# Attention: the value products in two row halves of 64 keys, set apart between the score products

## The chip, the cores and the metric

The kernel runs on one core of one Trainium2 chip. The metric is the time of one execution on the device, in microseconds, as the median of several runs. Engines are named as in the profile: PE is TensorE (PEld its weight loads), DVE is VectorE, ACT is ScalarE, POOL is GpSimd, SP is SyncE, which issues most of the DMAs.

## The reference, cut to what matters

```python
def _A_ref(x, wqkv, wo):                    # B=1, S=2048, D=640
    H = 32
    Dh = D // H                             # 20
    q, k, v = ...                           # x @ wqkv, each [B, H, S, Dh]
    scores = jnp.einsum("bhqd,bhkd->bhqk", q, k) * (Dh ** -0.5)
    p = _softmax(scores, axis=-1)
    o = jnp.einsum("bhqk,bhkd->bhqd", p, v)
    return (...o as [B, S, D]...) @ wo

x = A_x
h = x + _A_ref(_layernorm(x, axis=-1), A_wqkv, A_wo)
h2 = h + _B_ref(_layernorm(h, axis=-1), B_w_gate, B_w_up, B_w_down)   # swiglu, F=1728
```

All is float32. The change touches the attention alone, from the scores to the sums of `p` times `v`.

## The kernel before, in words

The program has three parts: layer norm with the q, k and v projections; attention; the output projection, second layer norm and feed-forward part. Some work of the third part (splitting weights on POOL, the first output projections) is put between attention steps.

Attention takes four heads at a time (`G = 4`, eight groups) and 512 queries at a time, which makes 32 *units* (`NU`). A unit goes over the 2048 keys in 16 *steps* of 128 keys, so there are 512 steps. Two heads are stacked on the rows of a tile: head rows 0 to 61 are the lower row half (`b = 0`), rows 64 to 125 the upper one (`b = 1`). A head has 20 columns; a product of 60 rows takes three pairs of split parts (high and low) of them at once, and two more rows subtract the maximum.

What a step does, by the names in the code:

- `scores` (L1290, L1296): four products of 62 rows by 512 queries, `s` for the lower row half and `S` for the upper. Each fills one PSUM bank (`ps_one`), and ACT takes the exponential of it into `probs`.
- `max_one` (L261, L267) and `max_start` (L289, L298): the maxima of the scores for a *later* unit. `m` and `M` are single products of 60 rows by 512 keys on one row half, each followed by a DVE reduction of its bank (`ps_max`). `x` and `X` are the two parts, 256 keys each, of one shared item: the lower half in `x`, the upper in `X` of the same step, into one bank, with one reduction for both after `X`. Of the items a third is shared (`EVERY = 3`). About 490 of the 512 steps have maxima to do; the last twenty or so have none left.
- `weigh` (L1300), called `W`: the sums of `probs` times values for the step two before, four heads in four column blocks of 32, over all 128 keys in one go. They are float32 products; the program holds four, and the chip runs eight instructions. They add up over a unit's 16 steps in one bank, `acc`.

The order of these operations on PE is written out by hand in a string, `ORDER = "WxnSmSsMXs"`; `n` is a marker on ACT that issues no work. Steps without maxima use `"sSsSW"`. There is no scheduler: each engine gets its instructions in the order of the code.

PSUM has eight banks: one for `acc`, four for scores (`ps_one` goes round two of the pool `psum_two` and two of the pool `psum`), three for maxima (`ps_max`).

At the end of a unit, which is in the second step of the next one, `row_sums` copies `acc` to SBUF on ACT (L1310) and sends its row sums off by DMA; the reciprocals and the scaling follow some steps later on DVE and POOL. `max_all` (L309) reduces the found maxima of a unit to one column, `found_of` (L277) makes the tile for them.

Of the kernel before, what the change touches and what calls it, by code (L numbers as in the profile page):

```python
# [9 lines left out]
F32 = mybir.dt.float32  # L10
# [7 lines left out]
P = 128  # L18
# [6 lines left out]
NT = S // P  # L25
# [15 lines left out]
ORDER = "WxnSmSsMXs"  # L41
# [7 lines left out]
EXTRA = 2  # L49
EVERY = 3  # L50
# [3 lines left out]
def tile_block(ctx: ExitStack, tc: tile.TileContext, x, wqkv, wo, wg, wu, wd, out):  # L54
# [218 lines left out]
    def found_of(u):  # L273

        if u not in found:
            f = found[u] = pp.tile([P, 2, 2, TPC, NC + EXTRA], F32, name="found", tag="found", bufs=3)
            nc.vector.memset(f[:, :, :, :, NC:], LOWEST)  # L277
# [4 lines left out]
    def max_start(u, kc, t, pair, half, column):  # L282

        ps = ps_max()

        def part(b):
            rows = slice(b * ROW, b * ROW + NPART)
            first = kc * CH + half * CH // 2
            nc.tensor.matmul(  # L289
                ps[:, b * CH // 2 : (b + 1) * CH // 2],  # L290
                queries[u][rows, pair, t * P : (t + 1) * P],
                keys[u // NC][rows, pair, first : first + CH // 2],
                start=(b == 0), stop=True, skip_group_check=True,
            )

        def last():
            part(1)
            nc.vector.tensor_reduce(  # L298
                found_of(u)[:, :, pair, t, column], ps.rearrange("p (b n) -> p b n", b=2),
                axis=AX.X, op=ALU.max,  # L300
            )

        part(0)
        return lambda: nc.scalar.clobber_nop([nc.scalar.lower_ap(ps)]), last
# [71 lines left out]

    plain_items, shared = [], []
    used = {}
    for n, (u, kc, t, pair) in enumerate(rest):
        if n % EVERY:  # L380
            plain_items.append((u, kc, t, pair))
        else:
            extra = NC + used.setdefault((u, t, pair), 0)
            used[u, t, pair] += 1
            shared += [(u, kc, t, pair, 0, kc), (u, kc, t, pair, 1, extra)]
    assert max(used.values()) <= EXTRA

# [910 lines left out]
    def weigh(u, kt, probs, acc):  # L1298
        for j in range(G):
            nc.tensor.matmul(  # L1300
                acc[32 * j : 32 * j + 32, :],
                values[u // NC][:, kt, j * VW : j * VW + 32],
                probs[j // 2][:, j % 2, :],
                start=(kt == 0), stop=(kt == NT - 1),
                tile_position=(0, 32 * j),
            )

    def row_sums(acc, *queues):
        o = pc.tile([P, CH], F32, name="o", bufs=2)
        nc.scalar.activation(o, acc, AF.Copy)  # L1310
# [36 lines left out]
    def counted(u):  # L1347
        left[u] -= 1
        if left[u] == 0:
            max_all(u)  # L1350
            if early_end(u):
                turn_maxima(u)
            closing[u] = now[0] + 2

    def next_max(b):
        if singles[b]:
            a = singles[b].pop(0)
            max_one(*a)
            counted(a[0])

    def next_shared(b):
        if b == 0 and shared:
            a = shared.pop(0)
            begun.append((a[0], *max_start(*a)))
        elif b == 1 and begun:
            u, _, last = begun.pop()
            last()
            counted(u)

    def weigh_next():  # L1370
        u, kt, probs = todo.pop(0)
        if kt == 0:
            accs[u] = psum.tile([P, CH], F32, name="acc", tag=f"ps_{last % 3}")
        weigh(u, kt, probs, accs[u])
        if kt == NT - 1:
            queues = [nc.sync] if u + 1 < NU else [nc.scalar, nc.sync]
            tail.append((u, *row_sums(accs.pop(u), *queues)))
# [3 lines left out]
    for u in range(NU):  # L1381
# [4 lines left out]
        for kt in range(NT):  # L1386
# [3 lines left out]
            order = ORDER if singles[0] or singles[1] or shared else "sSsSW"  # L1390
            place[0] += 1
            for op in order:
                if op in "mM":
                    next_max(int(op == "M"))
                elif op in "xX":
                    next_shared(int(op == "X"))
                elif op == "n":
                    if begun:
                        begun[0][1]()
                elif op in "sS":  # L1400
                    scores(u, kt, heads[op == "S"].pop(0), probs)
                else:
                    if len(todo) == 2:
                        weigh_next()
# [55 lines left out]
    while todo:  # L1460
        weigh_next()
# [562 lines left out]
```

## Time and profile before

| what | value |
|---|---|
| time, median of 2 runs | 2010.26 us (2009.89 to 2010.63) |
| the profiled execution | 2008.45 us, with a span of 2006.6 us |
| granted PE clock | 1.00 |
| PE busy | 99% of the span, 14792 instructions |
| PEld busy | 63% |
| DVE busy | 80%, 2873 instructions |
| ACT busy | 71%, 2833 instructions |
| POOL busy | 39% |
| DMA | 310.50 MB, mean 155 GB/s |
| first and last value product | 325.9 us and 1440.7 us after the start |

The attention steps thus fill some 1115 us of the 2006.6 us span. The ends of PE's products are modelled in the profile, so a PE that is shown 99% busy need not be at its peak; starts can be compared with each other. Two rows of one engine that overlap are pipelined: the next begins before the one ahead has ended.

### The profile page before, as it was taken

The numbers are of one execution on the slowest core, as the hardware profiler recorded it, in microseconds if no ns is written. First come the engines' busy times: TensorE is split into PE (matmuls) and PEld (weight loads), VectorE is DVE, ScalarE is ACT, GpSimd is POOL, SyncE is SP. The second block draws the span as 40 slices with busy tenths as digits, with TensorE's granted clock in tenths as the row PEclk, the third lists the DMA queues.
The fourth block names the chain that finished last, engine by engine and source line by source line (L and its number), as shares of the span: only waits on it lengthen the run. The fifth ranks groups of instructions, "written<-read, shape, count | busy, mean of one in ns | idle before, by whom it ended". The sixth has DMA issues, their size and how long they took to land.

```text
span 2006.6 us, 41982 instructions
## 1 busy us (share of the span) xinstructions
PE 1983.5 (99%) x14792; PEld 1261.6 (63%) x14792; DVE 1606.8 (80%) x2873; ACT 1433.0 (71%) x2833; POOL 784.4 (39%) x1147
## 2 busy tenths in 40 slices
PE   8999999999999999999999999999999999999998
PEld 6989996444444444444444444455688888888888
DVE  5687778999999999999999988975488666676667
ACT  4677778999999999999999999977633222212221
POOL 6564423243342343234342111011245544844465
PEclk9999999999999999999999999999999999999999
DMA  7787563442533443434334222221258645974542
GB/s 240 262 254 258 173 209 88 128 123 94 161 104 122 141 140 125 130 119 149 128 130 157 79 73 60 77 66 60 62 204 289 232 168 175 354 251 162 201 147 94
DMA packets 197066, 310.50 MB, mean 155 GB/s; under 512 B 51368, under 2 KB 85480, under 8 KB 195832
## 3 DMA queue, kind: packets, MB, share of 16 engines
q1 hardware_dynamic: 190264, 284.21, 43.7%
q0 software_dynamic: 6496, 23.60, 4.0%
q8 instruction: 118, 1.93, 0.4%
q14 instruction: 92, 0.75, 0.1%
q10 hardware_dynamic: 96, 0.00, 0.0%
HBM read 208.11 MB, written 99.19 MB: 153 GB/s over the span
## 4 chain that ended last, share of the span: by engine, by line
PE 88%; DMA 2%; DVE 1%; POOL 1%; issue 1%; ACT 0%; SPq 0%; DVEq 0%; ACTq 0%; POOLq 0%
PE acc L1300 25%; PE ps_a L1487 15%; PE ps_one L1290 12%; PE ps_max L289 9%; PE ps_b L1581 8%; PE ps_max L261 7%; PE ps_one L667 7%; PE ps_max L228 2%; PE ps_max L1021 2%; PE ps_b L1021 1%; DMA o_t<-o_d 0%; DMA units<-w_d 0%; DMA halves<-j_d 0%; DMA t_d<-kept 0%; PE ps_max L1056 0%
## 5 line engine op out<-in xcount | busy, mean ns | idle before, releaser
L1296 ACT ACTIVATE probs<-ps_one 128x512 f32<-128x512 f32 x2048 | 1048.9, 616 | 44.1 <-PE ps_one L1290 34.8
L267 DVE TENSOR_REDUCE found<-ps_max 128x1 f32<-128x512 f32 x980 | 630.5, 685 | 83.3 <-PE ps_max L261 63.7
L1290 PE MATMUL ps_one<-q_stk,k_stk 62*128 62x512 f32 x2048 | 577.4, 428 | 1.1 <-DVE m L102 0.9
L1300 PE MATMUL acc<-probs,v_stk 128*32 128x512 f32 x4096 | 545.2, 604 | 0.0
L289 PEld LDWEIGHTS ps_max<-k_stk,q_stk 60*128 60x128 f32 x984 | 181.8, 185 | 407.2 <-DVE found L267 400.3
L261 PE MATMUL ps_max<-k_stk,q_stk 60*128 60x512 f32 x980 | 392.7, 422 | 0.0
L298 DVE TENSOR_REDUCE found<-ps_max 128x2 f32<-128x512 f32 x492 | 335.3, 682 | 0.0
L289 PE MATMUL ps_max<-k_stk,q_stk 60*128 60x256 f32 x984 | 324.1, 329 | 0.0
L1290 PEld LDWEIGHTS ps_one<-q_stk,k_stk 62*128 62x128 f32 x2048 | 303.1, 184 | 25.3 <-ACT probs L1296 19.5
L1702 DVE TENSOR_TENSOR tmp<-ps_a,tmp 128x512 f32<-128x512 f32 x208 | 141.2, 689 | 120.4 <-PE ps_a L1487 93.6
L250 DVE TENSOR_REDUCE mx<-ps_max 128x2 f32<-128x512 f32 x288 | 180.4, 685 | 63.9 <-PE ps_max L228 60.0
L261 PEld LDWEIGHTS ps_max<-k_stk,q_stk 60*128 60x128 f32 x980 | 181.0, 185 | 50.2 <-DVE found L298 21.9
L240 ACT ACTIVATE ps_max<-ps_max 128x512 f32<-128x512 f32 x288 | 151.6, 583 | 46.4 <-PE ps_max L228 43.7
L1581 PE MATMUL ps_b<-halves,yp 128*128 128x320 f32 x1032 | 179.3, 308 | 2.0 <-DMA halves<-j_d 1.2
L1581 PEld LDWEIGHTS ps_b<-halves,yp 128*128 128x128 f32 x1032 | 165.1, 188 | 18.6 <-POOL yp L102 1.5
L1487 PE MATMUL ps_a<-t,units 128*128 128x512 f32 x624 | 162.5, 396 | 0.0
L1300 PEld LDWEIGHTS acc<-probs,v_stk 128*32 128x32 f32 x4096 | 80.6, 108 | 127.6 <-issue 118.5
L1487 PE MATMUL ps_a<-z,units 128*128 128x512 f32 x516 | 133.8, 394 | 0.0
L102 POOL TENSOR_TENSOR yp<-y,yp 128x256 fp32r<-128x256 f32 x96 | 60.4, 629 | 187.8 <-ACT yp L101 187.8
L1487 PEld LDWEIGHTS ps_a<-t,units 128*128 128x128 f32 x624 | 112.6, 188 | 18.6
L1335 POOL TENSOR_TENSOR o<-o,rb 128x512 f32<-128x512 f32 x31 | 40.0, 1289 | 200.9 <-DMA rb<-r_d 94.7
L1586 DVE TENSOR_TENSOR h<-ps_b,h 128x320 f32<-128x320 f32 x248 | 109.9, 480 | 6.9 <-PE ps_b L1581 5.4
(220 smaller groups left out, 2977.7 us busy)
## 6 DMA issues: line engine op xcount, KB each, us to landing
units<-w_d SPq DMA_DIRECT2D x186, 256.0 KB
w_d<-stage SPq DMA_DIRECT2D x106, 256.0 KB
halves<-j_d SPq DMA_DIRECT2D x70, 320.0 KB
j_d<-stage SPq DMA_DIRECT2D x42, 320.0 KB
k_stk<-k_d SPq DMA_DIRECT2D x64, 160.0 KB
q_stk<-q_d SPq DMA_DIRECT2D x64, 160.0 KB
raw<-k_d SPq DMA_DIRECT2D x62, 160.0 KB
raw<-q_d SPq DMA_DIRECT2D x54, 160.0 KB
```

The source lines that it names most:

```text
L240: nc.scalar.activation(ps, ps, AF.Relu)
L250: nc.vector.tensor_reduce(mx[:, b, :, t, kc], ps.rearrange("p (j n) -> p j n", j=2), axis=AX.X, op=ALU.max,)
L261: nc.tensor.matmul(ps, queries[u][rows, pair, t * P : (t + 1) * P], keys[u // NC][rows, pair, kc * CH : (kc + 1) * CH], start=True, stop=True,
L267: nc.vector.tensor_reduce(found_of(u)[:, b, pair, t, kc : kc + 1], ps, axis=AX.X, op=ALU.max)
L289: nc.tensor.matmul(ps[:, b * CH // 2 : (b + 1) * CH // 2], queries[u][rows, pair, t * P : (t + 1) * P], keys[u // NC][rows, pair, first : ...
L298: nc.vector.tensor_reduce(found_of(u)[:, :, pair, t, column], ps.rearrange("p (b n) -> p b n", b=2), axis=AX.X, op=ALU.max,)
L1290: nc.tensor.matmul(ps, keys[u // NC][rows, p, kt * P : (kt + 1) * P], queries[u][rows, p, :], start=True, stop=True,)
L1296: nc.scalar.activation(probs[p][:, b, :], ps, AF.Exp, scale=scale)
L1300: nc.tensor.matmul(acc[32 * j : 32 * j + 32, :], values[u // NC][:, kt, j * VW : j * VW + 32], probs[j // 2][:, j % 2, :], start=(kt == 0) ...
L1487: nc.tensor.matmul(ps.rearrange("p (t n) -> p t n", t=TPC), w[k][:, i], z[k][:, :, j], start=(first and m == 0), stop=(last and m == len(n ...
L1581: nc.tensor.matmul(ps, a, b, start=(n == 0), stop=(n == len(pairs) - 1))
L1702: add = lambda out, ps, x: nc.vector.tensor_tensor(out=out, in0=ps, in1=x, op=ALU.add)
```

## The change

Three things change together, all in the attention.

1. `weigh` gets a row half `b`. Its products take 64 keys instead of 128, and a second call does the other 64. `v` in the new order strings is the lower half, `w` the upper. The two halves add up in banks of their own, `acc0` and `acc1`, and `row_sums` adds the two on DVE after ACT's copy.
2. The shared items with their two parts of 256 keys go. All maxima are single products of 512 keys again, three in each step. The order string becomes two, for even and odd steps.
3. The second bank of sums is taken from the scores, which then have three banks; the maxima keep three.

```diff
-ORDER = "WxnSmSsMXs"
+ORDERS = ("SMvSswmsm", "smwsvSMSM")
...
-EXTRA = 2
-EVERY = 3
...
     def ps_one():
-        n = turn[0] % 4
+        n = turn[0] % 3
         turn[0] += 1
         if n < 2:
             return psum_two.tile([P, CH], F32, name="ps_one", tag="ps_two")
-        return psum.tile([P, CH], F32, name="ps_one", tag=f"ps_{(last + n - 1) % 3}")
+        return psum.tile([P, CH], F32, name="ps_one", tag=f"ps_{(last + 1) % 3}")
...
-    def weigh(u, kt, probs, acc):
+    def weigh(u, kt, probs, acc, b):
+        rows = slice(b * ROW, (b + 1) * ROW)
         for j in range(G):
             nc.tensor.matmul(
                 acc[32 * j : 32 * j + 32, :],
-                values[u // NC][:, kt, j * VW : j * VW + 32],
-                probs[j // 2][:, j % 2, :],
+                values[u // NC][rows, kt, j * VW : j * VW + 32],
+                probs[j // 2][rows, j % 2, :],
                 start=(kt == 0), stop=(kt == NT - 1),
-                tile_position=(0, 32 * j),
+                tile_position=(b * ROW, 32 * j),
             )
 
     def row_sums(acc, *queues):
         o = pc.tile([P, CH], F32, name="o", bufs=2)
-        nc.scalar.activation(o, acc, AF.Copy)
+        nc.scalar.activation(o, acc[0], AF.Copy)
+        nc.vector.tensor_tensor(out=o, in0=acc[1], in1=o, op=ALU.add)
...
-    singles = [[(*a, b) for a in plain_items] for b in range(2)]
-    begun = []
+    singles = [[(*a, b) for a in rest] for b in range(2)]
...
-    def weigh_next():
-        u, kt, probs = todo.pop(0)
-        if kt == 0:
-            accs[u] = psum.tile([P, CH], F32, name="acc", tag=f"ps_{last % 3}")
-        weigh(u, kt, probs, accs[u])
+    weighing = []
+
+    def weigh_next(b):
+        if not weighing:
+            weighing.append((todo.pop(0), {0, 1}))
+        (u, kt, probs), halves = weighing[0]
+        halves.remove(b)
+        if kt == 0 and len(halves) == 1:
+            accs[u] = [
+                psum.tile([P, CH], F32, name=f"acc{i}", tag=f"ps_{(last + 2 * i) % 3}")
+                for i in range(2)
+            ]
+        weigh(u, kt, probs, accs[u][b], b)
...
-            order = ORDER if singles[0] or singles[1] or shared else "sSsSW"
-            place[0] += 1
+            order = ORDERS[kt % 2] if singles[0] or singles[1] else "sSvsSw"
```

How this moves the instructions is seen best in the order in which they stand. First PE, in the middle of the attention, before: a little over one step. Each row is a line of the kernel, an operation and its tiles, with its count where rows repeat; `acc` is the bank of sums, `ps_one` a bank of scores, `ps_max` a bank of maxima.

```order
L1300 MATMUL acc<-probs,v_stk_146 32x512 x4
L289 MATMUL ps_max<-k_stk_145,q_stk 128x256
L1290 MATMUL ps_one<-q_stk,k_stk_145 128x512
L261 MATMUL ps_max<-k_stk_145,q_stk 128x512
L1290 MATMUL ps_one<-q_stk,k_stk_145 128x512 x2
L261 MATMUL ps_max<-k_stk_145,q_stk 128x512
L289 MATMUL ps_max<-k_stk_145,q_stk 128x256
L1290 MATMUL ps_one<-q_stk,k_stk_145 128x512
L1300 MATMUL acc<-probs,v_stk_146 32x512 x4
```

In a step before, the four value products stand together once, and eight score and maximum products stand between two such groups; the second of the two 256-key parts (L289) stands *ahead* of the step's last score product (L1290).

Now PE at the same place in the changed kernel, a little over one step, from the first value half of an even step on. L1252 is the score product, L259 the maximum, L1263 the value product; `acc_14219` is a unit's `acc0` (lower rows), `acc_14220` its `acc1` (upper rows).

```order
L1263 MATMUL acc_14219<-probs,v_stk_5610 32x512 x4
L1252 MATMUL ps_one<-q_stk,k_stk_5609 128x512 x2
L1263 MATMUL acc_14220<-probs,v_stk_5610 32x512 x4
L259 MATMUL ps_max<-k_stk_145,q_stk 128x512
L1252 MATMUL ps_one<-q_stk,k_stk_5609 128x512
L259 MATMUL ps_max<-k_stk_145,q_stk 128x512
L1252 MATMUL ps_one<-q_stk,k_stk_5609 128x512
L259 MATMUL ps_max<-k_stk_145,q_stk 128x512
L1263 MATMUL acc_14220<-probs,v_stk_5610 32x512 x4
L1252 MATMUL ps_one<-q_stk,k_stk_5609 128x512
L1263 MATMUL acc_14219<-probs,v_stk_5610 32x512 x4
```

The value products now stand in two groups of four in each step. The two groups of the upper rows have five products of the lower rows between them (L259 and L1252 in turn), and the two groups of the lower rows likewise have upper ones.

The second place is DVE at the end of a unit, where `o` is the tile that `row_sums` fills, `neg` the unit's maxima and `r` the row sums. Before:

```order
L267 TENSOR_REDUCE found<-ps_max 128x1 x2
L298 TENSOR_REDUCE found<-ps_max 128x2
L329 STREAM_TRANSPOSE turned<-both 128x32
L267 TENSOR_REDUCE found<-ps_max 128x1 x2
L298 TENSOR_REDUCE found<-ps_max 128x2
L267 TENSOR_REDUCE found<-ps_max 128x1 x2
L298 TENSOR_REDUCE found<-ps_max 128x2
```

and in the changed kernel:

```order
L282 TENSOR_REDUCE neg<-found 128x16
L265 TENSOR_REDUCE found<-ps_max 128x1 x4
L302 STREAM_TRANSPOSE turned<-both 128x32
L1274 TENSOR_TENSOR o<-acc_11927,o 128x512
L265 TENSOR_REDUCE found<-ps_max 128x1 x11
L1285 RECIPROCAL r<-r 128x16
L265 TENSOR_REDUCE found<-ps_max 128x1 x37
```

DVE keeps three reductions a step, all of one column now, and gets one addition for each unit (L1274) that stands in the row of reductions; in the second step of a unit one reduction is ahead of it and two are behind it.

More of the change, by code (lines that the diff above doesn't have):

```diff
@@ L275, in found_of @@
         if u not in found:
-            f = found[u] = pp.tile([P, 2, 2, TPC, NC + EXTRA], F32, name="found", tag="found", bufs=3)
-            nc.vector.memset(f[:, :, :, :, NC:], LOWEST)
+            f = found[u] = pp.tile([P, 2, 2, TPC, NC], F32, name="found", tag="found", bufs=3)
             if u in mxs:
@@ L280, in found_of @@
         return found[u]
[L282 to L304, printed above, removed]
     def max_all(u):
@@ L374, in tile_block @@
     ]
[L377 to L386, printed above, removed]
     evp_ctx = ExitStack()
@@ L1358, in next_max @@
             max_one(*a)
[L1359 to L1368, printed above, removed]
-    def weigh_next():
-        u, kt, probs = todo.pop(0)
-        if kt == 0:
-            accs[u] = psum.tile([P, CH], F32, name="acc", tag=f"ps_{last % 3}")
-        weigh(u, kt, probs, accs[u])
-        if kt == NT - 1:
-            queues = [nc.sync] if u + 1 < NU else [nc.scalar, nc.sync]
-            tail.append((u, *row_sums(accs.pop(u), *queues)))
+            u = a[0]
+            left[u] -= 1
+            if left[u] == 0:
+                max_all(u)
+                if early_end(u):
+                    turn_maxima(u)
+                closing[u] = now[0] + 2
+    weighing = []
[10 more added lines that the diff above has]
+        weigh(u, kt, probs, accs[u][b], b)
+        if not halves:
+            weighing.pop()
+            if kt == NT - 1:
+                queues = [nc.sync] if u + 1 < NU else [nc.scalar, nc.sync]
+                tail.append((u, *row_sums(accs.pop(u), *queues)))
     extra = []
@@ L1402, in tile_block @@
                 else:
-                    if len(todo) == 2:
-                        weigh_next()
+                    if len(todo) == 2 or weighing:
+                        weigh_next(int(op == "w"))
+                    if not once:
+                        continue
+                    once = False
                     for v, at in closing.items():
@@ L1460, in tile_block @@
     while todo:
-        weigh_next()
+        weigh_next(0)
+        weigh_next(1)
     u, o, r = tail.pop()
```

13 lines of the change are left out of this document (1 added, 12 removed).

## The prediction

> **What bounds the kernel now.** I read first the page's busy times, then a window over the attention steps, then the order of time of one step, then the groups and waits. Only the steps with maxima are looked at: 490 of the 512, since 980 single maxima go two to a step.
>
> ```profile
> PE 1983.5 (99%) x14792; PEld 1261.6 (63%) x14792; DVE 1606.8 (80%) x2873; ACT 1433.0 (71%) x2833; POOL 784.4 (39%) x1147
> L261 PE MATMUL ps_max<-k_stk,q_stk 60*128 60x512 f32 x980 | 392.7, 422 | 0.0
> 400.00:1300.00 900.00, 899.75 (x6875) 378.28 (x6871) 824.22 (x1409) 889.25 (x1754) 284.11 (x474) 1.00 0.39 118
> 400.00:1300.00 900.00, 877.51 (x1715) 1.00 0.39 118
> ```
>
> The third row is the window from 400 to 1300 us (busy time and count of PE, PEld, DVE, ACT, POOL), the fourth the same for the exponentials alone. Over the whole program ACT is 71% busy; in this window it is 889 of 900 us, DVE 824 and PE all of it. The whole-span shares hide that three engines are nearly full here. The 1715 exponentials, four to a step, make a step 900 × 4 / 1715 = **2.10 us**, and a unit of 16 steps 33.6 us.
>
> Which of the three is the bound? PE in order of time (start, length):
>
> ```profile
> 699.55 0.61 PE L1300 MATMUL acc<-probs,v_stk 128*32 128x512 f32 x4
> 700.10 0.38 PE L289 MATMUL ps_max<-k_stk,q_stk 60*128 60x256 f32 x1
> ...
> 701.22 1.07 PE L1300 MATMUL acc<-probs,v_stk 128*32 128x512 f32 x8
> 702.21 0.38 PE L289 MATMUL ps_max<-k_stk,q_stk 60*128 60x256 f32 x1
> 702.22 0.49 PE L1290 MATMUL ps_one<-q_stk,k_stk 62*128 62x512 f32 x1
> 702.44 0.40 PE L261 MATMUL ps_max<-k_stk,q_stk 60*128 60x512 f32 x1
> 702.55 0.52 PE L1290 MATMUL ps_one<-q_stk,k_stk 62*128 62x512 f32 x2
> 702.78 0.41 PE L261 MATMUL ps_max<-k_stk,q_stk 60*128 60x512 f32 x1
> 702.91 0.39 PE L1290 MATMUL ps_one<-q_stk,k_stk 62*128 62x512 f32 x1
> 703.03 0.27 PE L289 MATMUL ps_max<-k_stk,q_stk 60*128 60x256 f32 x1
> 703.24 1.06 PE L1300 MATMUL acc<-probs,v_stk 128*32 128x512 f32 x8
> 704.23 0.39 PE L289 MATMUL ps_max<-k_stk,q_stk 60*128 60x256 f32 x1
> ```
>
> From one value group to the next, 701.22 to 703.24, is 2.02 us: 0.99 us from the group's start to the next product, and 1.03 us in which the two row halves work side by side. The 0.99 us is always there (703.24 to 704.23 again): PE's own, not a wait. The first row shows a group's second four; from it to the next product is 0.55 us, so a pass of four takes 0.44 us, two take 0.89, and about **0.10 us** is spent going over to products of another shape. On entry the same: the last score started at 702.91 and, at the ordinary spacing on one half (702.55 to 702.78, 0.23 to 0.24 us), left its half at 703.14; the group began at 703.24.
>
> So PE needs at least 2.02 us a step and a step takes 2.10: **PE is the bound**. ACT stands close behind:
>
> ```profile
> 1333.13 2.06 ACT L1296 ACTIVATE probs<-ps_one 128x512 f32<-128x512 f32 x4 [1.27 <-PE ps_one L1290]
> L1296 ACT ACTIVATE probs<-ps_one 128x512 f32<-128x512 f32 x1715 | 878.0, 616 | 10.8 <-PE ps_one L1290 2.6
> 700.75 1.29 DVE L267 TENSOR_REDUCE found<-ps_max 128x1 f32<-128x512 f32 x2
> L267 DVE TENSOR_REDUCE found<-ps_max 128x1 f32<-128x512 f32 x858 | 552.3, 685 | 73.7 <-PE ps_max L261 56.2
> ```
>
> Four exponentials end 2.06 us after the first begins, and one lasts 0.616, so they follow each other at (2.06 − 0.62) / 3 = 0.48 us: 1.92 us a step. Two reductions take 1.29 us at 0.685 each, a spacing of 0.605: three take 1.82 us.
>
> **The change, inside a unit.** PE, for one row half in two steps: four scores and three maxima at 0.235 us, two value groups at 0.89, and two changes of shape (the half's two groups stand next to each other) at 0.10: 7 × 0.235 + 1.78 + 0.20 = 3.63 us, **1.81 us a step** instead of 2.02, if one half's value group runs beside the other half's scores. No row of before shows 64-key groups or such mixed work, so the 0.89 is that of 128 keys (the same 512 columns and eight instructions). Below, it can be no less than half of that by the rows, if half the keys took half the time, and then PE is only further from being the bound; above, it is the full serial price, priced as a rival.
>
> PE's instruction count grows: 7 + 16 = 23 products a step, against 16. The densest row that I found,
>
> ```profile
> 218.00:228.00 10.00, 10.00 (x158) 9.90 (x157) 6.77 (x12) 7.65 (x16) 6.22 (x7) 1.00 0.65 203
> ```
>
> has 158 products with their weight loads in 10 us, 63 ns each: 23 take 1.46 us, inside 1.81. At nothing, then, though a burst of eight behind a late bank can push a score by up to 0.5 us.
>
> With PE at 1.81, ACT is late next: 64 exponentials at 0.48 and the copy at the same spacing make 31.2 us a unit, 1.95 a step. DVE: 48 reductions at 0.605 are 29.0 us, and its small work is
>
> ```profile
> L309 DVE TENSOR_REDUCE neg<-found 128x16 f32<-128x96 f32 x27 | 6.9, 254 | 0.9
> L1321 DVE RECIPROCAL r<-r 128x16 f32<-128x16 f32 x27 | 6.5, 243 | 0.0
> L329 DVE STREAM_TRANSPOSE turned<-both 128x32 f32<-128x32 f32 x20 | 4.0, 201 | 0.0
> ```
>
> with three smaller groups some 0.9 us a unit; the new addition is nearest to the feed-forward part's addition from PSUM of the same shape, 0.69 us (below). Sum 30.6 us. So with every bank free in time a unit takes 31.2 us instead of 33.6, a gain of 2.4.
>
> Three score banks instead of four: a bank is taken for 0.39 (product) and 0.62 (exponential) and, by the gaps in these rows, about 0.15 between them and to the next product, 1.2 us; three at 0.48 give 1.44. Enough, with 0.2 us to spare, as long as nothing ahead is late. With the cover gone, each 0.1 us of lateness beyond that goes to ACT whole.
>
> **The end of a unit.** Here the change adds a wait. Before, the copy costs this:
>
> ```profile
> 727.42 0.63 ACT L1310 ACTIVATE o<-acc 128x512 f32<-128x512 f32 x1
> 728.11 1.06 PE L1300 MATMUL acc<-probs,v_stk 128*32 128x512 f32 x8
> L1702 DVE TENSOR_TENSOR tmp<-ps_a,tmp x208: 673/691/693, 1489.8 to 1993.4; 128x512 f32<-128x512 f32 x104
> ```
>
> The copy ends at 728.05 and the next unit's first group starts 0.06 us later. In the changed kernel the second step of a unit runs (from its start): score 0, maximum 0.24, score 0.47, value group of the lower rows 0.80, ending with its pipeline at 1.86; copy to 2.53; addition to 3.27. The addition waits in DVE's queue with two of the step's reductions behind it, and those hold two of the three banks of maxima. DVE has finished the step's first reduction at about 1.35, so it stands idle some 1.2 us. Its slack in a unit is only 31.2 − 30.6 = 0.6. The maxima of the next step wait for those banks, and on PE the scores behind them. And the upper rows' first group of the new unit, which stands about 1.0 us into the third step (2.95), waits for the addition (3.3).
>
> I price this between nothing (31.2 us a unit) and twice the 1.4 us from group's end to addition's end, once for DVE and once for PE behind it (34.0). DVE's idle time less its slack alone gives 31.8. I take **1.5 us**, just over the one-way length, so 32.7 us a unit.
>
> Other moves, at nothing: the row-sum DMAs are issued behind the addition, 0.7 us later in SP's queue, with stores and later units' queries behind them; the reciprocals that need them stand three steps on, 6 us, and queries are loaded three units ahead, so both keep their cover. The memset of 85 ns a unit goes. The twenty-odd steps without maxima have the same products with groups halved; their score parts are short, and I put them at 0 ± 6 us (20 steps by a third of a group's 0.89).
>
> **Sum**: 490 / 16 = 30.6 units × (33.6 − 32.7) = 27.5 us, 2008.45 − 27.5 = 1981 against the profiled execution. The median is 1.8 us above that execution, so 1983. With the ends, 31.4 to 34.0 us a unit, the time would be 1943 to 2022; I use 1955 as the lower end, since no unit will be free of the wait.
>
> **Rivals.** *The shapes exclude each other.* If PE finishes all work of one shape, on both halves, before it begins another, nothing overlaps. In favour: 0.10 us is lost at each change of shape in the rows above. Against: there both sides of the change share rows, so they do not tell whether a half by itself may change. The price: in two steps six products stand one after another on the upper rows (1.41 us), a score on each half (0.24), five on the lower (1.18) and one more (0.24), with four groups at 0.99 and four entries at 0.10: 7.43 us, 3.71 a step. (3.71 − 2.10) × 490 = 789 us, so **2800 us**. It decides as soon as a group of one half cannot start while the other half streams. [...]
>
> *Products start strictly in the order of the program.* Then a half's product waits for the start of all ahead of it, other half or not. Followed through: S 0, M 0.24, v 0.24, s 1.22 with w, then m, s, m, s, m to 2.40, w 2.40, s 2.63, v 2.97, then S 3.39, M, S, M, and the next S at 4.33: 2.165 a step, +32 us, and with the unit's end on top up to +78: 2042 to 2088, about **2065 us**. Against it: in the fence above the score at 702.91 starts before the 256-key maximum at 703.03, which the program puts ahead of it; the maximum's half was still taken, and the score passed it. [...]
>
> *Nothing is won* because the wait at the unit's end takes all 2.4 us: 2010 us. It is the upper part of my own range.
>
> **How the numbers follow.** My forecast, halves that run independently with a unit at 31.4 to 34.0 us: 0.68. Strict order: 0.12. Shapes exclude each other: 0.16. Anything else near no change, such as the two halves' streams slowing each other by a tenth: 0.04. A measurement of this kernel tells about 2%, 40 us, from no change. Faster by more needs a unit under 32.3 us, a third of my case: 0.22. Slower by more: all of the exclusion, nearly all of strict order, and 0.02 of mine: 0.29. Between: 0.49. The range takes in my case and the strict order, 1955 to 2085, and leaves out the exclusion and the tails, together 0.2. My own case alone is 1955 to 2022.
>
> **What will show it.** Right: L1263 groups with starts inside the other half's L1252 and L259 rows; ordinary steps near 1.95 us with exponentials 0.48 apart; a step of over 2.5 us once a unit, at L1274, with DVE waiting for L1273. Wrong: no product between the starts of a group and 0.9 us later (exclusion); scores never ahead of an earlier product of the other half (strict order); ACT idle within units, waiting for scores (too few banks).

## The result, and the profile after

The changed kernel takes **4436.49 us**, before 2010.26 us: a ratio of 2.207 (95% interval 2.197 to 2.216). The page of the changed kernel, with the row of the granted clock in 40 slices:

```profile
span 4434.6 us, 48244 instructions
PE 4411.8 (99%) x18396; PEld 1958.3 (44%) x18396; DVE 1713.0 (39%) x2874; ACT 1583.1 (36%) x2833; POOL 778.8 (18%) x1147
PEclk9995555555555555555555555555555556999999
L1258 ACT ACTIVATE probs<-ps_one 128x512 f32<-128x512 f32 x2048 | 1189.1, 597 | 2278.2 <-PE ps_one L1252 2276.7
```

PE is shown 99% busy, as before, and ACT has gone from nearly full in the attention to waiting 2277 us for scores. The clock row is new: 1.0 before the attention and after it, **0.5 in nearly all of it**. (It comes back at 3726 us, 143 us before the last value product and 5.7 us after the first full-array products of the output projection, at 3720.3.) Two windows, before the attention and in it, and the exponentials alone from 400 to 3600 us:

```profile
200.00:300.00 100.00, 98.63 (x1226) 94.29 (x1224) 73.87 (x118) 76.81 (x153) 35.28 (x46) 1.00 0.59 190
400.00:500.00 100.00, 100.00 (x330) 32.45 (x322) 30.08 (x47) 33.27 (x57) 13.27 (x25) 0.50 0.21 64
400.00:3600.00 3200.00, 1052.39 (x1804) 0.50 0.12 35
```

1804 exponentials in 3200 us make a step 7.10 us, against 2.10. PE in order of time, some three quarters of a step (the dots stand for two more single products):

```profile
1500.01 0.79 PE L1252 MATMUL ps_one<-q_stk,k_stk 62*128 62x512 f32 x1
1500.73 1.93 PE L1263 MATMUL acc<-probs,v_stk 64*32 64x512 f32 x8
1502.59 0.79 PE L1252 MATMUL ps_one<-q_stk,k_stk 62*128 62x512 f32 x1
1503.18 0.62 PE L259 MATMUL ps_max<-k_stk,q_stk 60*128 60x512 f32 x1
1503.61 0.62 PE L1252 MATMUL ps_one<-q_stk,k_stk 62*128 62x512 f32 x1
1504.03 0.62 PE L259 MATMUL ps_max<-k_stk,q_stk 60*128 60x512 f32 x1
...
1505.44 1.93 PE L1263 MATMUL acc<-probs,v_stk 64*32 64x512 f32 x8
```

Two things are to be read here. No score or maximum starts between a group's start (1500.73) and 1.86 us later, though the six that follow are of the other row half: the halves do not overlap here. And the singles follow at 0.43 us, where it was 0.235: the half clock. The clock falls at the very start of the attention, before the first value product:

```profile
323.97 0.50 PE L1252 MATMUL ps_one<-q_stk,k_stk 62*128 62x512 f32 x1 [0.90 <-ACT probs L1258]
325.76 0.40 PE L259 MATMUL ps_max<-k_stk,q_stk 60*128 60x512 f32 x1
326.00 0.58 PE L1252 MATMUL ps_one<-q_stk,k_stk 62*128 62x512 f32 x1
326.38 0.63 PE L259 MATMUL ps_max<-k_stk,q_stk 60*128 60x512 f32 x1
```

From 326 us on a product is shown at 0.63 instead of 0.39 us; two microseconds earlier PE had stood idle for 0.90 us behind ACT. That this wait took the clock is not shown. The kernel before has a wait of 0.19 us there and a clock of 1.00 throughout; in a later run of it, with bare products added behind the attention, the clock falls at the same place all the same, and is back 3.4 us later:

```profile
326.10:329.40 3.30, 3.30 (x20) 1.55 (x16) 1.58 (x3) 2.33 (x5) 3.25 (x2) 0.50 0.75 243
329.50:1441.00 1111.50, 1110.25 (x8349) 482.09 (x8341) 971.42 (x1693) 1065.68 (x2106) 317.84 (x514) 1.00 0.36 108
```

So it is not the fall that sets the changed kernel apart, but that the clock does not come back.

### The profile page after: what moved, and what is told of

Read it like the earlier page. It is cut to its first block, busy times and chain, and to the rows that moved or that the text cites. A ratio compares the mean times of both kernels' runs of the same rounds, so it can differ in the third digit from the quotient of the medians.

```text
span 4434.6 us, 48244 instructions
## 1 busy us (share of the span) xinstructions
PE 4411.8 (99%) x18396; PEld 1958.3 (44%) x18396; DVE 1713.0 (39%) x2874; ACT 1583.1 (36%) x2833; POOL 778.8 (18%) x1147
## 4 chain that ended last, share of the span: by engine, by line
PE 95%; DVE 1%; POOL 0%; DMA 0%; issue 0%; ACT 0%; SPq 0%; DVEq 0%; POOLq 0%; ACTq 0%
PE acc L1263 42%; PE ps_one L1252 22%; PE ps_max L259 16%; PE ps_a L1448 7%; PE ps_b L1542 4%; PE ps_one L629 3%; PE ps_max L226 1%; PE ps_max L983 1%; PE ps_b L983 1%; DMA halves<-j_d 0%; PE ps_max L1018 0%; DVE tmp L1663 0%; POOL h L1580 0%; PE ps_a L1812 0%; DVE h L1547 0%
## 5 line engine op out<-in xcount | busy, mean ns | idle before, releaser
L1258 ACT ACTIVATE probs<-ps_one 128x512 f32<-128x512 f32 x2048 | 1189.1, 597 | 2278.2 <-PE ps_one L1252 2276.7
L1263 PE MATMUL acc<-probs,v_stk 64*32 64x512 f32 x8192 | 1915.5, 1027 | 0.2 <-ACT o L1273 0.2
L265 DVE TENSOR_REDUCE found<-ps_max 128x1 f32<-128x512 f32 x1472 | 1015.5, 691 | 2249.5 <-PE ps_max L259 2248.7
L1252 PE MATMUL ps_one<-q_stk,k_stk 62*128 62x512 f32 x2048 | 1207.9, 694 | 1.0 <-ACT probs L1258 0.9
L1252 PEld LDWEIGHTS ps_one<-q_stk,k_stk 62*128 62x128 f32 x2048 | 533.5, 297 | 1300.6 <-issue 1197.3
L259 PE MATMUL ps_max<-k_stk,q_stk 60*128 60x512 f32 x1472 | 951.4, 647 | 0.0
L259 PEld LDWEIGHTS ps_max<-k_stk,q_stk 60*128 60x128 f32 x1472 | 466.3, 317 | 498.6 <-issue 397.8
L1263 PEld LDWEIGHTS acc<-probs,v_stk 64*32 64x32 f32 x8192 | 198.1, 134 | 539.0 <-issue 518.7
L629 PE MATMUL ps_one<-z_hi,w_lo 64*128 64x512 f32 x380 | 112.5, 393 | 0.0
L629 PE MATMUL ps_one<-z_hi,w_hi 64*128 64x512 f32 x380 | 111.7, 393 | 0.0
L629 PE MATMUL ps_one<-z_lo,w_hi 64*128 64x512 f32 x380 | 111.2, 392 | 0.0
```

The source lines that it names most:

```text
L259: nc.tensor.matmul(ps, queries[u][rows, pair, t * P : (t + 1) * P], keys[u // NC][rows, pair, kc * CH : (kc + 1) * CH], start=True, stop=True,
L265: nc.vector.tensor_reduce(found_of(u)[:, b, pair, t, kc : kc + 1], ps, axis=AX.X, op=ALU.max)
L629: nc.tensor.matmul(ps, a[rows], b[rows], start=(i == n == 0), stop=(i == 1 and n == last), skip_group_check=True,)
L1252: nc.tensor.matmul(ps, keys[u // NC][rows, p, kt * P : (kt + 1) * P], queries[u][rows, p, :], start=True, stop=True,)
L1258: nc.scalar.activation(probs[p][:, b, :], ps, AF.Exp, scale=scale)
L1263: nc.tensor.matmul(acc[32 * j : 32 * j + 32, :], values[u // NC][rows, kt, j * VW : j * VW + 32], probs[j // 2][rows, j % 2, :], start=(kt ...
```

## The experiments

The first rival, exclusion, had foretold serial groups, but 2800 us, not 4436. So two questions were open: what excludes what, and why the clock is halved. Runs labelled *stretches* are the kernel before with bare products added after the attention, whose results nobody reads; their stretches are read by windows. The other runs are variants of the changed kernel.

**Bare stretches behind dense work.** The edit, in short (`LO`, `HI`, `ALL` are the row halves and all rows; `warm` is 60 full-array products):

```diff
+    def mm(i, rows, cols, n=0):          # one-pass products, as the scores are
+        nc.tensor.matmul(bank[i][cols, :], wo_hi[rows, n % 4, cols], wo_hi[rows, 4, :CH], ...)
+    def four(i, rows, row, kt):          # one value group: four blocks of 32 columns
+        ...
+    for stretch in (rows64, rows64x2, rows96, cols64, cols32, low, both, whole, mixed):
+        warm()
+        stretch()
```

A product of `mm` is in the number format of the scores (fp32r in the kernel) and one instruction in the trace. It is called *one-pass* from here on, as a name for the format alone. A float32 value product is two instructions.

> The kernel before with nine stretches of bare PE products added after the attention, each behind 60 products that fill the array; nothing reads their results. In order: 170 products of 64 lower rows by 128 columns; 170 such pairs, lower and upper rows in turn; 170 of 96 rows; 170 of 128 rows by 64 columns; 170 of 128 rows by 32 columns; 40 value groups of the lower 64 keys; 40 pairs of lower and upper groups; 40 groups of all 128 keys; 20 lower groups each with four products of the upper rows. Theory A (PE does one tile shape at a time, and the clock is granted by how much of the array is in use): the 64-row stretch and the lower groups fall to a clock of 0.50, so 170 products take some 70 us instead of 40 and 40 groups some 70 us instead of 36; the paired stretches and the whole groups stay at 1.00 (40, 36 and 36 us); the mixed stretch falls and has no product of the upper rows beside a group. Theory B (the clock falls because of the many changes of shape and their drains): every stretch but the mixed one stays at 1.00. Theory C (a group of 64 keys is slow by itself): lower groups take over 0.89 us at a clock of 1.00, and pairs twice that.

Five of its nine windows: 64 rows alone, 128 rows by 32 columns, lower groups alone, pairs of groups, mixed.

```profile
1457.00:1495.00 38.00, 38.00 (x168) 30.84 (x168) 0.00 (x0) 0.00 (x0) 0.00 (x0) 1.00 0.00 0
1667.00:1706.00 39.00, 39.00 (x170) 18.31 (x169) 0.00 (x0) 0.00 (x0) 0.00 (x0) 1.00 0.00 0
1720.00:1754.00 34.00, 34.00 (x317) 10.06 (x320) 0.00 (x0) 0.00 (x0) 0.00 (x0) 1.00 0.01 1
1768.00:1802.00 34.00, 34.00 (x632) 12.16 (x638) 0.00 (x0) 0.00 (x0) 0.00 (x0) 1.00 0.01 2
1865.00:1907.00 42.00, 42.00 (x240) 16.35 (x240) 0.00 (x0) 0.00 (x0) 0.00 (x0) 1.00 0.00 1
```

Every stretch kept a clock of 1.00 over its 34 to 42 us, half the array idle or not, mixed or not. So theory A's clock, as I had put it, falls, and so does B's. A lower and an upper group run side by side (632 products in the 34 us in which lower groups alone make 317), at 0.86 us a group or pair: theory C falls. The mixed stretch does exclude, at full clock, in order of time:

```profile
1870.34 1.19 PE L1467 MATMUL bank<-wo_hi 64*128 64x512 f32 x4
1871.46 1.06 PE L1474 MATMUL bank<-probs,v_stk 64*32 64x512 f32 x8
1872.45 1.18 PE L1467 MATMUL bank<-wo_hi 64*128 64x512 f32 x4
```

From a group's start to the next product is 0.99 us and from there to the next group 1.12: 2.11 us a round, where side by side it would be about 0.9 (four 64-row products in a row take 4 × 0.226).

**Value halves next to each other.**

```diff
-ORDERS = ("SMvSswmsm", "smwsvSMSM")
+ORDERS = ("vwSmsMSms", "vwsMSmsMS")
...
-            order = ... else "sSvsSw"
+            order = ... else "vwsSsS"
```

> The changed kernel with the two value halves next to each other (orders vwSmsMSms and vwsMSmsMS, and vwsSsS without maxima): still 64-key groups in two banks, three score banks, single maxima, the addition on DVE. Theory A: the two groups run side by side in 0.89 us, the clock stays at 1.00, two changes of shape a step as before: a step of 2.02 to 2.15 us, 1990 to 2050 us in all. Theory B: the same, 1990 to 2050. Theory C: groups of 64 keys do not run side by side or are slow: a step of at least 3.0 us, 2450 us or more.

It took 2324.16 us (1.155 of before, 1.153 to 1.158), at a clock of 0.993. That fits no theory. Its trace, in order of time:

```profile
900.43 0.50 PE L1252 MATMUL ps_one<-q_stk,k_stk 62*128 62x512 f32 x1
900.97 2.06 ACT L1258 ACTIVATE probs<-ps_one 128x512 f32<-128x512 f32 x4 [0.57 <-PE ps_max L259]
901.62 0.49 PE L1252 MATMUL ps_one<-q_stk,k_stk 62*128 62x512 f32 x1 [0.21 <-ACT probs L1258]
902.04 1.09 PE L1263 MATMUL acc<-probs,v_stk 64*32 64x512 f32 x16
904.67 0.66 PE L1263 MATMUL acc<-probs,v_stk 64*32 64x512 f32 x8
```

All sixteen value instructions, both halves, are done in the time of eight (1.09 us, against 1.06 in the mixed stretch). What is late is the step's fourth score (901.62): it waits for the bank of the first (900.43), whose exponential starts at 900.97 and lasts 0.6 us. A bank cycle of 1.19 us has to fit into the 1.03 us that the scores have between two groups. So three score banks cost here, and two runs took that apart: whole groups of 128 keys and single maxima, with four score banks and with three.

```diff
# both: the changed kernel, weigh() over all 128 rows into one bank, no addition
+ORDERS = ("vSmsMSms", "vsMSmsMS")
# four banks only:
-        n = turn[0] % 3
+        n = turn[0] % 4
```

> Only the second part of the change: whole value products of 128 keys in one bank, four score banks and three for maxima as before, and all maxima as single products, two on one half and one on the other in turn, with the halves in turn (orders vSmsMSms and vsMSmsMS). PE has 0.99 + 4 x 0.235 + 0.10 = 2.03 us a step, as before with its shared items. All theories: 2000 to 2025 us, the same as before within 1%.

> The kernel of whole value groups and single maxima in turn that took 2037 us, with three banks of scores instead of four, and nothing else changed. It is also the run with adjacent halves of 64 keys (2324 us) with whole groups in their place. If three banks of scores cost that run its time: 2300 us, within 1% of it. If the groups of 64 keys do: 2040 us.

Four banks: 2037.36 us (1.014, 1.012 to 1.016). Three: 2275.83 us (1.131, 1.128 to 1.135). In the window from 500 to 1200 us the steps are 2.15 and 2.61 us by the counts of exponentials, first with four banks, then with three:

```profile
500.00:1200.00 700.00, 670.32 (x1300) 1.00 0.39 122
500.00:1200.00 700.00, 552.35 (x1071) 1.00 0.34 105
```

So the fourth bank is worth 238 us where value groups come in one block, and giving up the shared maxima, with the order of products that goes with it, costs 27 us, a little more than the 1% I allowed. The run with groups of 64 keys side by side, and the addition on DVE, took 2324 − 2276 = 48 us on top. Not all of that is the groups' own: its clock was 0.993 against 0.999, and in the same window its 1062 exponentials make a step 2.637 us, against 2.614. A version with adjacent halves, four score banks and two of maxima was to check this:

```diff
+            return psum.tile([P, CH], F32, ..., tag=f"ps_{(last + 1) % 3}" if n == 2 else "ps_max2")
...
-        return psum.tile([P, CH], F32, name="ps_max", tag=f"ps_max{place[0] % 3}")
+        return psum.tile([P, CH], F32, name="ps_max", tag=f"ps_max{place[0] % 2}")
```

> The value halves next to each other as before, but with four banks of scores and two of maxima instead of three and three. The trace of the run with three showed the fourth score of a step waiting for the first one's exponential, 1.19 us after that score, and so 2.63 us a step. If the score banks set the time: 2.05 to 2.2 us a step, 1990 to 2070 us, unless two banks of maxima now do the same to the maxima (a bank is taken for 0.43 + 0.68 us and 0.1 more, so two allow three maxima in 1.8 us: 2.2 us a step, 2070 us). If the halves in groups of 64 keys are what costs: 2320 again.

2536.43 us (1.262, 1.254 to 1.269), a miss: PE now waits for the two banks of maxima (182 us between 500 and 1200 us), and its clock was 0.94 in that window, 0.968 over the run. It says nothing clean about the halves.

**Apart, but with both halves' products in turn between the groups.**

```diff
+ORDERS = ("vSmsMwSms", "vsMSmwsMS")
```

> The changed kernel with the value halves still apart, but with scores and maxima of the two row halves in turn between them (orders vSmsMwSms and vsMSmwsMS), four changes of shape a step as in the changed kernel. Theory A: two lone groups of 0.99 us and 1.03 us of paired products and two more entries of 0.10: 3.2 us a step at full clock, 2550 us; a third of the time the array is full, so the clock may hold or not; at 0.50 it is 6.4 us a step and 4100 us. Theory B: as many changes of shape as in the changed kernel, so the clock falls: 4100 us. If groups of one half did run beside products of the other after all: 2000 us.

3943.57 us. The exponentials from 500 to 3200 us:

```profile
500.00:3200.00 2700.00, 973.40 (x1791) 0.50 0.13 40
```

That is 6.03 us a step at 0.50, near the 6.4 foretold for that clock with exclusion. Without it the step would be some 4.2 us, an estimate: twice the 2.10 us of the kernel before. Pairing saves 1.07 us a step against the changed kernel and does not save the clock.

**Whole groups, scores and maxima grouped by half.**

```diff
+ORDERS = ("vSMSsmsm", "vsmsSMSM")       # whole groups, three score banks
```

> The changed kernel with its value products whole again (128 keys in one group, one bank, no addition), at the start of each step, but with scores and maxima grouped by row half as in the changed kernel (orders vSMSsmsm and vsmsSMSM). It tells how far products of one half pass waiting ones of the other. If they pass freely: 0.99 + 4 x 0.235 + 0.10 = 2.03 us a step or a little more, 1990 to 2060 us at a clock of 1.00. If they pass by no more than one or two: the halves stand one behind the other in part, up to 0.99 + 7 x 0.235 + 0.10 = 2.7 us, up to 2310 us at full clock; theory A then lets the clock fall if too little of the array is in use, theory B keeps it at 1.00.

2394.09 us at a clock of 0.997, above both expected ranges; the three banks are in it, and the rest was not taken apart. What it was for shows in the order of time:

```profile
900.13 0.51 PE L1252 MATMUL ps_one<-q_stk,k_stk 62*128 62x512 f32 x2
900.47 0.41 PE L259 MATMUL ps_max<-k_stk,q_stk 60*128 60x512 f32 x2
```

Two scores start within 0.01 us of each other (0.51 us for both, 0.50 for one), so one is upper and one lower, and likewise the two maxima. The program puts the first score of the second half fourth, behind two scores and a maximum of the first. Products of like shape thus passed at least two waiting ones of the other half here; strict order is out.

**Full-array bursts in the changed kernel.** With the theories of the clock fallen, a new one: the clock is caught low at the start and the kernel's own work, just busy enough to keep a full clock, cannot win it back.

```diff
+            if kt == 8 and u in (8, 20):
+                ps = ps_one()
+                for n in range(60):
+                    nc.tensor.matmul(ps, keys[g][:, 0, ...], keys[g][:, 1, :CH], start=True, stop=True)
```

> The changed kernel with 60 products of the full array put in at two places, in the ninth step of units 8 and 20 (into a bank of scores that nobody reads): 26 us each at half clock. It asks whether the clock of 0.50 belongs to the changed kernel's steady work or was only caught at the start of the attention, where PE stands idle for a few microseconds, and never given back. Theory D (caught): PE's steady work with its drains is busy enough to keep a clock of 1.00 and not enough to win it back; a burst wins it back and it then stays at 1.00, with steps of 3.5 to 3.8 us instead of 6.9, from unit 8 to the end: 8 units at 6.9 us a step, 24 at 3.7: 2.0 x 445 + 24 x 59 + 890 = 3190 to 3300 us. Theory E (steady): the clock falls back within some ten microseconds of each burst: 4440 to 4490 us.

3660.43 us. Windows before the first burst, after it, and after 1685 us, then one after the second burst:

```profile
900.00:1000.00 100.00, 100.00 (x327) 32.78 (x324) 29.47 (x45) 32.67 (x56) 13.38 (x25) 0.50 0.17 52
1300.00:1400.00 100.00, 100.00 (x594) 37.26 (x597) 49.96 (x82) 57.27 (x106) 16.59 (x31) 1.00 0.19 57
1690.00:1790.00 100.00, 100.00 (x325) 33.09 (x325) 30.40 (x48) 33.27 (x57) 7.84 (x13) 0.50 0.13 40
2700.00:2800.00 100.00, 100.00 (x594) 36.51 (x586) 50.09 (x87) 58.30 (x109) 7.60 (x7) 1.00 0.12 31
1300.00:1680.00 380.00, 211.84 (x390) 1.00 0.22 67
```

The same instructions run at either clock: 0.50 until the burst, then 1.00 (380 us in the last row). The last row, exponentials alone, gives 3.90 us a step at full clock. At 1685 us it fell back, and behind the second burst it was 1.00 in the windows taken, from 2350 to 2900 us. PE has no gap before the fall. A product of yet another kind stands 0.9 us ahead of it, the transpose of a unit's maxima (L318), which comes once in a few units:

```profile
1684.05 0.39 PE L259 MATMUL ps_max<-k_stk,q_stk 60*128 60x512 f32 x1
1684.36 0.28 PE L318 MATMUL ps_one<-ident,neg 128*16 128x128 f32 x1
1685.23 1.93 PE L1263 MATMUL acc<-probs,v_stk 64*32 64x512 f32 x8
```

That it was the cause is not borne out. The changed kernel has nine of them from 398 to 3786 us, one in 3.7 units. At 3.90 us a step that makes one in some 230 us, an estimate, so another should stand in the 380 us of the last row and two in the 500 us from 2400 to 2900, and the clock was 1.00 over both. What took it at 1685 us is open. Theory D holds, except that the full clock did not last.

**The same stretches behind an idle PE.**

```diff
+    def idle():
+        for n in range(24):
+            nc.scalar.activation(bank[0], bank[0], AF.Relu)
...
+        warm(); idle(); stretch()
```

> The kernel before with stretches of bare products after the attention, as in the first such run, but each put behind an idle PE (24 passes of ACT over a bank, 14 us), save for a first one behind dense products. In order: 30 times a group of the lower 64 keys and four products of the upper rows (behind dense products, then four stretches behind idle PE): 170 products of 64 rows; 40 groups of the lower 64 keys; the same 30 mixed rounds; 30 rounds of a whole group and four products on each half; 40 whole groups. Theory D: all that are dense come back to 1.00 within some 10 us of their start (some 45 us for each of the three dense ones); the first mixed stretch stays at 1.00 with 2.1 us a round, while the same stretch behind an idle PE stays at 0.50 with 4.0 us a round or more. Theory E: both mixed stretches have the same clock.

Windows: mixed behind dense work; then behind idle: 64 rows, lower groups, mixed, and the paired rounds (a whole group and four products on each half; from 4.6 us after their start).

```profile
1457.00:1519.00 62.00, 62.00 (x356) 23.71 (x348) 0.00 (x0) 0.00 (x0) 0.00 (x0) 1.00 0.00 1
1549.00:1621.00 72.00, 72.00 (x169) 55.25 (x170) 0.00 (x0) 0.00 (x0) 0.00 (x0) 0.50 0.00 0
1653.00:1720.00 67.00, 67.00 (x316) 15.05 (x312) 0.00 (x0) 0.00 (x0) 0.00 (x0) 0.50 0.00 1
1740.00:1867.00 127.00, 115.19 (x359) 40.38 (x360) 0.00 (x0) 11.16 (x20) 0.00 (x0) 0.50 0.00 0
1903.00:1963.00 60.00, 60.00 (x458) 23.25 (x450) 0.00 (x0) 0.00 (x0) 0.00 (x0) 1.00 0.00 1
```

The mixed rounds take 2.11 us a round at 1.00 or 3.86 at 0.50, by what stood ahead: the same work ran at two lasting speeds. The paired rounds (1.00) and, last, whole groups alone (0.95 in their window) won it back. I had expected the dense 64-row stretches to win the clock back, and they did not in 72 and 67 us without a gap. So dense work on half the rows *kept* the clock (1.00 over 38 us, in the first such run) and did not *win* it back (0.50 over 72 us).

**Which work wins it back, and which shapes exclude.**

```diff
+    for stretch in (rows96, cols64, cols32, rows64x2, both):     # behind idle
...
+    def unlike_cols():  ...  mm(0, LO, ALL, n); mm(1, HI, slice(0, 64), n)
+    def unlike_rows():  ...  mm(0, LO, ALL, n); mm(1, slice(ROW, ROW + 32), ALL, n)
```

> The kernel before with stretches of bare products after the attention. Five stand behind an idle PE (14 us), to see which work wins the clock back: 170 products of 96 rows; 170 of 128 rows by 64 columns; 170 of 128 rows by 32 columns; 170 pairs of lower and upper 64 rows; 40 pairs of lower and upper value groups of 64 keys. Two stand behind dense products, to see whether any two unlike shapes exclude each other on different row halves: 100 pairs of 64 lower rows by 128 columns and 64 upper rows by 64 columns; 100 pairs of 64 lower rows by 128 columns and 32 upper rows by 128 columns. If the clock counts rows in use: the pairs of halves win it back within 20 us (about 45 us a stretch), 128 rows by few columns do too, 96 rows may or may not. If it counts the whole array's cells: 128 rows by 64 or 32 columns stay at 0.50 (72 us a stretch). If shapes exclude each other: the unlike pairs take at least 2 x 0.23 us and their changes, 0.6 to 0.7 us a pair; if only value groups are excluded, 0.23 us a pair.

Windows: 96 rows, 128 rows by 32 columns, pairs of 64 rows (all behind idle); unlike columns, unlike rows (behind dense work).

```profile
1472.00:1512.00 40.00, 40.00 (x168) 32.81 (x168) 0.00 (x0) 0.00 (x0) 0.00 (x0) 0.94 0.00 0
1611.00:1652.00 41.00, 41.00 (x168) 18.88 (x167) 0.00 (x0) 0.00 (x0) 0.00 (x0) 0.93 0.00 0
1682.00:1721.00 39.00, 39.00 (x335) 38.12 (x334) 0.00 (x0) 0.00 (x0) 0.00 (x0) 0.97 0.00 1
1800.00:1822.00 22.00, 22.00 (x193) 20.32 (x195) 0.00 (x0) 0.00 (x0) 0.00 (x0) 1.00 0.01 1
1838.00:1976.00 138.00, 138.00 (x196) 54.19 (x195) 0.00 (x0) 0.00 (x0) 0.00 (x0) 0.51 0.00 0
```

The first three come back (0.94, 0.93 and 0.97 in their windows; if they began at 0.50, that is 2 to 6 us of it, an estimate), a quarter of the array's columns being enough here with all rows in use; so do the two left out here, 128 rows by 64 columns (0.96) and pairs of value groups (0.97). Of these shapes it is rows that count: 96 won it back, and 64, in the run before, did not. Of the unlike pairs, 128 against 64 columns run side by side (193 products in 22 us, 0.23 us a pair). 64 against 32 rows exclude each other: 196 products in 138 us are 1.41 us a pair, where two products one after the other take 0.86 at half clock (0.43 each, above). With no gap in PE's work the clock was even lost: 1.00 in the stretch ahead, a mean of 0.51 in this one.

**What in a value group excludes.** Value groups are unlike the scores in three ways: blocks of 32 columns, blocks that do not begin at column 0, and float32.

```diff
+    def plain32():     mm(0, LO, ALL, n); mm(1, HI, slice(0, 32), n)
+    def beside(place, weights):          # one float32 product above, four one-pass ones below
+        nc.tensor.matmul(bank[1][place, :], weights(...), pr[HI, 0, :], tile_position=(ROW, place.start), ...)
+        for m in range(4): mm(0, LO, ALL, m)
```

> The kernel before with five stretches of bare products after the attention, each behind dense full-array products. [...] In order: 100 pairs, lower 64 rows by 128 columns and upper 64 rows by 32 columns at column 0, both one-pass; then 30 rounds each of one float32 product on the upper rows and four one-pass products on the lower: the float32 product with 128 columns; with 32 columns at column 0; with 32 columns at column 32; last, 30 of the float32 products of 128 columns alone. A float32 product alone is expected at 0.86 us. If the width of the blocks excludes: the pairs take 0.6 us or more, the rounds with 128 columns 0.93 us, the other two 2.0 us. If the number format excludes: the pairs take 0.23 us and all three rounds 2.0 us. If the column place excludes: only the round at column 32 takes 2.0 us.

Windows: the one-pass pairs, then rounds with a float32 product of 128 columns, of 32 at column 0, of 32 at column 32.

```profile
1457.00:1479.00 22.00, 22.00 (x195) 19.85 (x193) 0.00 (x0) 0.00 (x0) 0.00 (x0) 1.00 0.01 1
1494.00:1521.00 27.00, 27.00 (x179) 23.35 (x180) 0.00 (x0) 0.00 (x0) 0.00 (x0) 1.00 0.01 1
1536.00:1597.00 61.00, 61.00 (x176) 23.40 (x176) 0.00 (x0) 0.00 (x0) 0.00 (x0) 1.00 0.00 0
1612.00:1674.00 62.00, 62.00 (x179) 23.68 (x178) 0.00 (x0) 0.00 (x0) 0.00 (x0) 1.00 0.00 0
```

Neither the number format (27 us for 30 rounds, 0.90 each: the two instructions of a float32 product, which start 0.43 us apart there, run beside four one-pass products of 0.23) nor the place of the columns (61 and 62 us alike) excludes by itself. A float32 product in a block of 32 columns does, 2.08 us a round at column 0 and 62 us for the 30 rounds at column 32. A one-pass product of 32 columns at column 0 does not (195 products in 22 us, 0.23 us a pair). Why those two differ is open: the float32 products are also given their place in the array (`tile_position`) and the one-pass ones are not, and other placements of one-pass blocks were not tried.

## Why the prediction was wrong

**What bounds the kernel** before, PE with ACT and DVE just behind, fits the runs, though none tested it apart; the run with three banks shows how little the score banks had to spare.

**"If one half's value group runs beside the other half's scores"** is the step that failed. It did not: from a group's start to the next product it was 0.99 us in the mixed stretch and 1.86 in the changed kernel, and the 1.81 us a step that I worked from it was 3.90 at full clock. The exclusion, which I gave 0.16, is what happened, at a price near the one I had worked out (3.71); what that left out is the first single product behind each group, 0.59 us to the next instead of 0.43 in the changed kernel's order of time above. I had named the 0.10 us lost at each change of shape in its favour, and given more weight to what the rows of before leave open. The runs show exclusion for blocks of 32 float32 columns (2.08 us a round) and for 32 against 64 rows (1.41 us a pair at half clock), and not for every difference of block width: 128 against 64 columns ran side by side at 0.23 us a pair.

**The clock** was in no term. I took 1.00 from the page and priced every variant at it, the exclusion too: 2800 us. By the measured steps I estimate (3.90 − 2.10) × 490 = 882 us for the exclusion and (7.10 − 3.90) × 490 = 1568 us for the clock, together 2450, against a measured 2426. The clock's part is nearly twice that of the exclusion, and hangs on it: with one half working at a time, PE did not win the clock back once it had fallen at the attention's start (0.50 from 326 to 3726 us), where the kernel before, in the run in which it fell, had it back in 3.4 us. What makes it fall there is open. Being busy was not enough to bring it back: 170 products on 64 rows without a gap ran for 72 us at 0.50.

**Three score banks, "enough, with 0.2 us to spare"**: I had checked the bank cycle (1.2 us; 1.19 measured) only against scores that flow evenly. Where value groups of 1.0 us stand in one block the scores have only the rest of the step, and three banks cost 238 us. In the changed kernel this is hidden behind PE, whose weight loads for the scores wait for banks 1.5 us in all from 400 to 3720 us.

**The single maxima** had no term of their own in the sum; they cost 27 us, together with the new order of the products, in the run that kept whole groups and four banks. **The end of a unit**, my 1.5 us of waiting, and with it the DVE bound, could not be seen: with a step of 7.10 us instead of 2.10 DVE and ACT have time to spare.

**Strict order** was rightly held unlikely: like-shaped products passed those of the other half (two scores of different halves 0.01 us apart, with two products between them in the program).

No run points to a version better than the kernel before. Groups whole and in one block, with four banks of scores, are what the two halves' exclusion asks for, and the shared maxima are worth their trouble.

## What to carry to other kernels

Two row halves of TensorE did not overlap for every pair of shapes here: 64×64 beside 64×128 did (0.23 us a pair), float32 blocks of 64×32 beside 64×128 did not (2.08 us a round). Before splitting a product to fill the other half, run the two shapes side by side bare, for it takes one stretch of some 40 us. Read the granted clock of each stage, and ask of a change not only how busy PE will be but how many rows it keeps at work: the stage that used half of them at a time here lost its clock and did not win it back for 3400 us (0.50 from 326 to 3726 us). Count banks against the stretch in which their products can be issued, not against the whole step.

## What the runs showed of the hardware that I had not expected

- The same instructions ran at two lasting speeds: 7.10 us a step in the changed kernel (clock 0.50), 3.90 behind a burst of full-array work (1.00).
- The clock was kept by dense work on 64 rows (1.00 over 38 us) and not won back by it (0.50 over 72 us); 96 rows (0.94 in their window), two halves of 64 in turn (0.97), and 128 rows by only 32 columns (0.93) all won it back. It was lost without a gap in PE's work by 64 rows in turn with 32 (a mean of 0.51 over 138 us).
- Two value groups of 64 keys on the two halves took the time of one (632 products in 34 us against 317).
- A float32 product of 128 columns ran beside one-pass products of the other half at full rate (0.90 us a round), one of 32 columns did not (2.08 us).
